# Keys of ten attention units transposed in 32 x 32 blocks by VectorE, and weight conversions started one chunk earlier

## The chip, the cores and the metric

The kernel runs on one core of a Trainium2 chip. The core has a matrix engine (TensorE, in the profile PE, with its weight loads as PEld), VectorE (DVE), ScalarE (ACT), GpSimd (POOL) and a queue engine (SyncE, SP) that here only issues DMAs; 16 DMA engines carry the transfers. TensorE writes into eight banks of PSUM, and VectorE or ScalarE take the results from there to SBUF. The metric is the device time of one execution in microseconds (us), the median of several runs.

## The reference

Everything is float32 at the boundary. Eight batches, 576 tokens, 8 heads of 64: a packed attention, then two mixing layers.

```python
p_packed = sm_attn(p, k, v)             # 32 packed queries p read 576 keys k
out = sm_attn(q, p_packed, p_packed)    # 576 queries q read the 32 packed rows
# sm_attn: softmax(q k^T / 8) v
x = out as [8, 576, 512]
xk, xr = mixes of x and of x one token earlier, by mu_k and mu_r
k = max(xk @ w_k, 0); v = (k * k) @ w_v; r = sigmoid(xr @ w_r); x = r * v
h = (x^T @ U @ V)^T; u = x + h
out = u + max(u @ w_ch1, 0) @ w_ch2     # 512 -> 2048 -> 512
```

The float64 weights (w_k, w_v, w_r, U, V, w_ch1, w_ch2) are converted to float32 on the chip, from their raw 64-bit words.

## The kernel before

**Attention units.** The batches go in four pairs, the heads in four pairs: 16 units, u = 4 * pair + head pair, each with two batches and two heads. A unit needs the keys K and queries Q with the 64 head dimensions on partitions, while a plain load puts tokens there. `attention_steps` (L664) works one unit: K into `kh` (and its last 64 tokens into `kt`), the packed queries into `pT`, scores of p against K, their exponentials `a1`, a product with V (`vin`), the packed result `pp`, then Q against `pp`, a second softmax `a2`, and the output `xo`, which is stored to `x_d` in DRAM.

There are two ways to turn an operand. The first is TensorE's transpose against the identity (`plan.transpose`, L207), 128 x 128 at a time into PSUM, and a copy out of PSUM by ScalarE or VectorE. The second is VectorE's transpose (`plan.turn`, L214), which transposes each 32 x 32 block in place; the load then has to bring the blocks to the right partitions, in pieces of 32 floats (128 B). `NPLAIN` (L522) is 8: units 0 to 7 turn K and Q by TensorE. In units 8 to 15 Q is already turned by VectorE (two transposes of 128 x 576) and `load_q` (L628) uses eight DMAs of 72 KB in 128-byte pieces; their final products run as three passes in a rounded format with zero-padded operands (`wide`) instead of full float32, and the second scores are computed transposed (`psat<-qt,ppt`). K is turned by TensorE in all 16 units: eight transposes of 128 x 128 and two of 64 x 128, two copies of 128 x 512 and one for the tail. `load_k` (L612) uses two DMAs of 256 KB and two of 32 KB.

**Chunks.** Phase 1 of the mixing layers runs in 12 chunks of 384 columns, three a pair of batches: `psr` (receptance), then eight `psk` and eight `psv` blocks, each product in three passes of a high and a low half. Chunks 0 to 2 read the output of units 0 to 3, chunks 3 to 5 that of units 4 to 7, and so on: the first chunk of a pair cannot start before its four units are stored and loaded again. Units 0 to 3 run alone at the start; the other twelve run between the chunks' matmuls. **Phase 2** (`psc`) is the last layer.

**Conversions.** `Cast.run` (L886) takes one [128, 512] block of 64-bit weights by one DMA of 512 KB into one of three buffers (`st`) and converts it with seven or eight instructions on ScalarE and VectorE. The weights of phase 1 (`wr`, `wk`, `wv`) are converted during the start and chunk 0, the last of them (`wv5` to `wv7`) just ahead of their use. The 34 blocks of U's partner V, `w_ch1` and `w_ch2` for phase 2 follow from the third chunk on, five a chunk (`CAST0, NPER = 2, 5`, L1385). From chunk 7 on `make_ws` (L1206) combines them into the operands of phase 2.

**Order.** All operations are first listed with their dependencies. `Plan.emit` (L346) then goes through them with modelled durations and writes, for each engine, one fixed order: the ready operation of the best class first, then by age or readiness. On the chip each engine runs its own order and waits at the head of its queue. In SP's order each DMA also waits for the DMA issued eight before it. A big buffer of a unit (`kin`, `qin`, `vin`, `kh`, `qt`, `at`, `th`, `xo`: eight, each reused one unit later) is loaded for unit u + 1 as soon as unit u has used it.

Of the kernel before, what the change touches and what calls it, by code (L numbers as in the profile page):

```python
# [9 lines left out]
F32 = mybir.dt.float32  # L10
# [3 lines left out]
AF = mybir.ActivationFunctionType  # L14
# [470 lines left out]
def packed_attention_moe_mixer_kernel(  # L485
# [18 lines left out]
    B, H, S, D = q.shape  # L504
    NP = p.shape[2]
    P = 128
    DM = H * D
    NJ = DM // P
# [10 lines left out]
    LATER = "v0 v1 v2 k0 k1 k2 k3 v3 v4 v5 v6 v7"  # L519
    NLEAD = NJ  # L520
    FIRST = "k0 p0 q0 w0 k1 v0 w1 q1 v1 w2 k2 q2 w3 v2 k3 w4 q3 v3 w5 w6 w7"
    NPLAIN = 2 * NJ  # L522
    SCALE = 1.0 / float(D) ** 0.5
    PASS = ((0, 0), (0, 1), (1, 0))

# [1 line left out]
    plan = Plan(nc)  # L527
# [37 lines left out]
    def ps_att():  # L565
        return plan.bank(att_banks[0], "psat", att_banks[0] is ps_a)
# [17 lines left out]
    class Bufs:  # L584
# [22 lines left out]
            return self.kept[1:]  # L607

        def tile_in(self, tag):
            return plan.tile(self.big_p, [P, 1152], F32, "big", parts=tuple(range(8)), name=tag)  # L610

        def load_k(self, u, after=()):  # L612
            bp, j = divmod(u, NJ)
            if u not in self.kin:
                self.kin[u] = self.tile_in("kin")
            t = self.kin[u]
            for b2 in range(2):
                src = k[2 * bp + b2, 2 * j:2 * j + 2]
                plan.dma(
                    t.at(b2)[:, b2 * 512:(b2 + 1) * 512].rearrange("p (h t d) -> p h t d", t=4, h=2),  # L620
                    src[:, 0:512, :].rearrange("h (p t) d -> p h t d", t=4), after=after)
            for b2 in range(2):
                src = k[2 * bp + b2, 2 * j:2 * j + 2]
                plan.dma(
                    t.at(2 + b2)[b2:P:2, 1024:1152].rearrange("p (h d) -> p h d", h=2),
                    src[:, 512:576, :].rearrange("h s d -> s h d"), after=after)

        def load_q(self, u, after=()):  # L628
# [3 lines left out]
            t = self.qin[u]  # L632
            if u >= NPLAIN:
                for b2 in range(2):
# [29 lines left out]
    def attention_steps(A, u, u_next):  # L664
        bp, j = divmod(u, NJ)
        kin, qin, vin = A.kin.pop(u), A.qin.pop(u), A.vin.pop(u)
        if j == 0 and bp + 1 < NBP:
            load_p(bp + 1)
        plan.copy(A.pbd, p_t[bp][:, j, :].unsqueeze(1).to_broadcast([P, 2, D]))
        plain = u < NPLAIN  # L670
        kh = A.big(F32, "kh")
        qt, at = A.big(F32, "qt"), A.big(F32, "at", (0, 1))
        pT, ppz = A.keep(plain)
# [5 lines left out]
        if early:  # L679
            claim()  # L680

        for b2 in range(2):
            yield
            ps = ps_att()
            for n in range(4):
                plan.transpose(ps[:, n * P:(n + 1) * P],
                               kin.at(b2)[:, b2 * 512 + n * P:b2 * 512 + (n + 1) * P], ident)
            plan.copy(kh[:, b2 * 512:(b2 + 1) * 512], ps)
        yield
        ps = ps_att()  # L690
        for h in range(2):
            plan.transpose(ps[0:64, h * P:(h + 1) * P], kin[:, 1024 + h * 64:1088 + h * 64], ident)
        plan.transpose(ps[:, 2 * P:3 * P], A.pbd.rearrange("p h d -> p (h d)"), ident)
        kt = at.at(1)[:, 640:896].rearrange("p (h c) -> p h c", h=2)
        plan.copy(kt[0:64].rearrange("p h (b c) -> p h b c", b=2),
                  ps[0:64, 0:2 * P].rearrange("p (h c b) -> p h b c", h=2, b=2))
        plan.copy(pT, ps[:, 2 * P:3 * P].rearrange("p (b c) -> p b c", b=2))
        if early:
            A.load_k(u_next, A.after)
# [1 line left out]
        st = A.st  # L701
        yield
        sps = [ps_att() for _ in range(2)]
        for b2 in range(2):
            for h in range(2):
                o = slice(b2 * 64 + h * 32, b2 * 64 + (h + 1) * 32)
                for r in range(2):
                    rows = slice(r * 64, (r + 1) * 64)
                    plan.mm(sps[r][o, 0:256], pT[rows, b2, h * 32:(h + 1) * 32],
                            kh[rows, b2 * 512 + h * 256:b2 * 512 + (h + 1) * 256],  # L710
                            start=True, stop=True, skip_group_check=True)
        for b2 in range(2):
            for h in range(2):
                o = slice(b2 * 64 + h * 32, b2 * 64 + (h + 1) * 32)
                plan.mm(sps[0][o, 256:320], pT[0:64, b2, h * 32:(h + 1) * 32],
                        kt[0:64, h, b2 * 64:(b2 + 1) * 64], start=True, stop=True, skip_group_check=True)
        s0, s1 = st.at(0), st.at(1)
        plan.reduce(s0[:, 0:1], sps[0][:, 0:320], ALU.max)
        plan.reduce(s0[:, 1:2], sps[1][:, 0:256], ALU.max)
# [1 line left out]
        a1 = A.a1  # L721
        bias = st.at(0)[:, 3:4]
        for r in range(2):
            plan.act(a1[:, 0:512].rearrange("p (n r c) -> p n r c", n=2, r=2)[:, :, r, :],
                     sps[r][:, 0:256].rearrange("p (n c) -> p n c", n=2), AF.Exp,
                     st.at(1)[:, 4 + r:5 + r], bias, SCALE)
        for b2 in range(2):
            r = slice(b2 * 64, (b2 + 1) * 64)
            plan.act(a1[r, 512 + b2:640:2], sps[0][r, 256:320], AF.Exp,
                     st.at(1)[r, 6:7], bias[r], SCALE)  # L730
        plan.reduce(s0[:, 8:9], s1[:, 4:8], add)
        plan.recip(s0[:, 9:10], s0[:, 8:9])

        for c in range(3 if plain else 0):
            yield
            ps = ps_att()
# [3 lines left out]
            n = 3 if c < 2 else 2  # L740
# [6 lines left out]
        if not plain:  # L747
            yield
            for b2 in range(2):
                r = slice(b2 * S, (b2 + 1) * S)  # L750
# [5 lines left out]
        ps = ps_att()  # L756
# [4 lines left out]
        ps = ps_att()  # L761
# [4 lines left out]
        ps = ps_att()  # L766
        for t in range(5):
            for g in range(4):
                o = t * P + g * 32
# [3 lines left out]
                        start=(t == 0), stop=(t == 4), skip_group_check=True)  # L773
# [3 lines left out]
        if not plain:  # L777
            for b2 in range(2):
                r = slice(b2 * 64, (b2 + 1) * 64)
# [5 lines left out]
        ps = ps_att()  # L785
# [13 lines left out]
        if plain:  # L799
# [25 lines left out]
            ps = ps_att()  # L825
# [4 lines left out]
            ps = ps_att()  # L830
            plan.transpose(ps[:, 0:P], a2f[:, 512:640], ident)
            for b2 in range(2):
                r = slice(b2 * 64, (b2 + 1) * 64)
                plan.copy(th[r, 512:576], ps[r, r])
        else:
            n = S // NP
            a2 = plan.tile(A.one, [P, 20, NP], F32, "a2", parts=(0, 1))[:, 0:n, :]
            s2 = plan.tile(A.one, [P, 4, 20], F32, "s2", parts=(0, 1))
            for g, (c0, c1) in enumerate(halves):
                yield  # L840
                ps = ps_att()
# [19 lines left out]
        for c0, c1 in halves:  # L861
            w = c1 - c0
            if plain:
                yield
                pss = [ps_att() for _ in range(2)]
                for b2 in range(2):
                    r = slice(b2 * 64, (b2 + 1) * 64)
# [13 lines left out]
    def attention(A, u, u_next):  # L881
        for _ in attention_steps(A, u, u_next):
            pass
# [83 lines left out]
    for what in FIRST.split():  # L967
        u = int(what[1])
# [14 lines left out]
    plan.cls = 0  # L983
    A0.after = go
    steps = [attention_steps(AX_[u], u, NJ if u == 0 else None) for u in range(NLEAD)]
    step = 0
    while any(s is not None for s in steps):
# [36 lines left out]
    for b2 in range(2):  # L1024
        r = slice(b2 * 64, (b2 + 1) * 64)
# [7 lines left out]
    for i0, i1 in ((0, NI),):  # L1033
        src = uv[:, i0 * NP:i1 * NP]
# [145 lines left out]
    def tmp_tile():  # L1180
        i = count["tmp"] % 6
        count["tmp"] += 1
        if i < 3:
            return plan.tile(m_p, [P, CW], F32, "m", name="tmp")[:, 0:256]
        return plan.tile(tr_p, [P, 256], F32, "tmp")
# [148 lines left out]
    def product(q, f, i, name, fresh):  # L1334

        if fresh:
            bank_abc[name] = plan.bank(ps_c1, "psc1")
        ps = bank_abc[name][:, 0:256]
        w, x = load_ws(f, i), ops[q][i]
        n = 0  # L1340
        for k in range(2):
            for wi, a in PASS:
                plan.mm(ps, half(w, wi)[:, k * P:(k + 1) * P],
                        half(x, a).rearrange("p (a k c) -> p k a c", a=4, k=2)[:, k],
                        start=(fresh and n == 0), stop=(n == 5), skip_group_check=True)
                n += 1
        return ps
# [34 lines left out]
            plan.dma(v_d[:, c * 288:(c + 1) * 288], w[0:NP, 0:288])  # L1382
        casts.append((slice(0, NP), V[:, c * 288:(c + 1) * 288], 288, put_v))
    NCAST, FIRST_WS = 9, 7
    CAST0, NPER = 2, 5  # L1385
    for m in range(MC):
        def put1(w, m=m):
            plan.dma(w1_d[m], w)
# [16 lines left out]
    for n in range(len(chunks)):  # L1405
        b, c = chunks[n]
# [27 lines left out]
        if n >= CAST0:  # L1434
            plan.cls = 3
            for _ in range(len(casts) if n == NCAST else NPER):
                if casts:
                    rows, src, size, put = casts.pop(0)
# [27 lines left out]
    for q in range(NQ):  # L1466
# [12 lines left out]
        for f in range(NF):  # L1479
# [9 lines left out]
            b = product(q, f, 1, "b", True)  # L1489
            s = tmp_tile()  # L1490
            plan.tt(s, p1, b, add)
            c = product(q, f, 2, "c", True)
# [68 lines left out]
```

## Time and profile before

| what | value |
|---|---|
| median of 3 runs | 1471.89 us (1470.66 to 1473.28) |
| profiled execution, its own time | 1469.44 us |
| span of that execution on the core | 1467.7 us |
| PE busy | 1434.1 us, 98% |
| PEld busy | 1259.5 us, 86% |
| DVE busy | 988.5 us, 67% |
| ACT busy | 716.2 us, 49% |
| mean granted TensorE clock | 0.988 |

1.74 us of the profiled execution lie outside its span. The page's slices show TensorE at 90% or more from the fourth slice to the last but one; a busy share is summed over modelled ends of pipelined matmuls, so it says that the engine had work, not how dense that work was. How dense is read from the distance between the start of a group of instructions and the start of the next group.

### The profile page before, as it was taken

The numbers are of one execution on the slowest core, as the hardware profiler recorded it, in microseconds if no ns is written. First come the engines' busy times: TensorE is split into PE (matmuls) and PEld (weight loads), VectorE is DVE, ScalarE is ACT, GpSimd is POOL, SyncE is SP. The second block draws the span as 40 slices with busy tenths as digits, with TensorE's granted clock in tenths as the row PEclk, the third lists the DMA queues.
The fourth block names the chain that finished last, engine by engine and source line by source line (L and its number), as shares of the span: only waits on it lengthen the run. The fifth ranks groups of instructions, "written<-read, shape, count | busy, mean of one in ns | idle before, by whom it ended". The sixth has DMA issues, their size and how long they took to land.

```text
span 1467.7 us, 25586 instructions
## 1 busy us (share of the span) xinstructions
PE 1434.1 (98%) x9104; PEld 1259.5 (86%) x9104; DVE 988.5 (67%) x2147; ACT 716.2 (49%) x1519; POOL 268.8 (18%) x519
## 2 busy tenths in 40 slices
PE   6799999999999999999999999999999999999998
PEld 5678888888888988889899999899998999999997
DVE  6999577888788888885665465556546554554533
ACT  5777656776666677664443333333223332333322
POOL 0000000000000000100333333333333333333331
PEclk8889999999999999999999999999999999999999
DMA  8864355666552877841999988899998789879763
GB/s 232 254 193 123 97 137 137 188 175 179 158 158 94 291 246 248 255 153 59 308 261 249 225 231 215 212 258 225 230 230 212 204 220 247 208 215 237 202 179 79
DMA packets 235709, 294.53 MB, mean 201 GB/s; under 512 B 91200, under 2 KB 126336, under 8 KB 235584
## 3 DMA queue, kind: packets, MB, share of 16 engines
q1 hardware_dynamic: 163008, 160.76, 37.8%
q0 software_dynamic: 72576, 132.15, 35.6%
q8 instruction: 73, 1.20, 0.3%
q14 instruction: 52, 0.43, 0.1%
HBM read 231.94 MB, written 60.89 MB: 200 GB/s over the span
## 4 chain that ended last, share of the span: by engine, by line
PE 90%; DMA 3%; DVE 3%; SPq 2%; ACT 1%; issue 1%; DVEq 0%; ACTq 0%
PE psc L197 50%; PE psk L197 13%; PE psv L197 13%; PE psr L197 7%; PE psat L197 4%; PE psat L209 2%; SPq L319 2%; PE psu L197 1%; DMA kin<-in_k_dram 1%; PE psh L197 1%; DMA st<-in_moe_w_k_dram 1%; DMA ut<-uq_d 0%; DMA st<-in_moe_w_v_dram 0%; DMA uq_d<-ux 0%; DMA w_d<-m 0%
## 5 line engine op out<-in xcount | busy, mean ns | idle before, releaser
L197 PE MATMUL psc<-w,hid 128*128 128x512 f32 x1728 | 421.1, 391 | 0.4 <-DVE hid L273 0.4
L197 PEld LDWEIGHTS psc<-ob,wb 128*128 128x128 f32 x3024 | 387.4, 191 | 13.4
L197 PE MATMUL psc<-ob,wb 128*128 128x256 f32 x3024 | 392.0, 283 | 0.0
L319 POOL DMA_DIRECT2D wb<-ws_d x504 | 266.9, 530 | 647.6 <-PE psc L197 401.5
L197 PEld LDWEIGHTS psc<-w,hid 128*128 128x128 f32 x1728 | 314.6, 188 | 60.6 <-DVE hid L273 1.5
L233 ACT ACTIVATE hid<-tmp 128x256 fp32r<-128x256 f32 x216 | 131.5, 676 | 231.0 <-DVE tmp L254 231.0
L197 PE MATMUL psk<-xk,wk 128*128 128x384 f32 x1152 | 227.1, 340 | 0.4 <-ACT sq L233 0.4
L197 PE MATMUL psv<-wv,kk 128*128 128x512 f32 x864 | 226.3, 397 | 0.0
L197 PEld LDWEIGHTS psk<-xk,wk 128*128 128x128 f32 x1152 | 201.3, 188 | 11.1 <-issue 2.6
L197 PEld LDWEIGHTS psv<-wv,kk 128*128 128x128 f32 x864 | 158.6, 188 | 32.9 <-issue 3.0
L273 DVE SCALAR_TENSOR_TENSOR hid<-tmp,hid 128x256 fp32r<-128x256 f32 x216 | 127.2, 633 | 54.6 <-ACT hid L233 54.1
L273 DVE SCALAR_TENSOR_TENSOR hid<-psc,hid 128x256 fp32r<-128x256 f32 x72 | 45.3, 629 | 167.4 <-ACT hid L233 167.4
L254 DVE TENSOR_TENSOR tmp<-tmp,psc 128x256 f32<-128x256 f32 x288 | 112.9, 409 | 61.7 <-PE psc L197 61.7
L233 ACT ACTIVATE hid<-psc 128x256 fp32r<-128x256 f32 x72 | 45.8, 636 | 157.3 <-PE psc L197 157.3
L197 PE MATMUL psr<-wr,xr 128*128 128x512 f32 x432 | 114.5, 406 | 2.0 <-DVE xr L291 1.6
L197 PEld LDWEIGHTS psr<-wr,xr 128*128 128x128 f32 x432 | 81.9, 194 | 21.3 <-DVE xr L291 2.1
L288 ACT ACTIVATE tmp<-psc 128x256 f32<-128x256 f32 x144 | 57.2, 397 | 58.7 <-PE psc L197 50.7
L233 ACT ACTIVATE sq<-psk 128x384 f32<-128x384 f32 x96 | 46.8, 489 | 75.1 <-PE psk L197 74.7
L311 POOL MEMSET x<- 128x8 f32 x4 | 0.4, 112 | 429.7 <-DVE m L270 249.2
L254 DVE TENSOR_TENSOR kk<-sq,kk 128x384 fp32r<-128x384 f32 x96 | 52.6, 549 | 25.1 <-ACT kk L288 24.6
L233 ACT ACTIVATE m<-x,om_t 128x384 f32<-128x384 f32 x96 | 55.3, 607 | 4.9 <-DVE xr L254 3.8
L270 DVE SCALAR_TENSOR_TENSOR m<-x,mu_t,m 128x384 f32<-128x384 f32 x96 | 56.4, 608 | 0.3 <-ACT m L233 0.2
(157 smaller groups left out, 1500.6 us busy)
## 6 DMA issues: line engine op xcount, KB each, us to landing
wb<-ws_d POOLq DMA_DIRECT2D x504, 256.0 KB, 4.0
st<-in_moe_w_ch_dram SPq DMA_DIRECT2D x32, 512.0 KB, 5.3
ws_d<-wb SPq DMA_DIRECT2D x56, 256.0 KB, 4.0
x_d<-xo SPq DMA_DIRECT2D x16, 576.0 KB, 3.8
x_d<-x SPq DMA_DIRECT2D x36, 256.0 KB, 2.6
kin<-in_k_dram SPq DMA_DIRECT2D x32, 256.0 KB, 4.5
vin<-in_v_dram SPq DMA_DIRECT2D x32, 256.0 KB, 4.8
x<-x_d SPq DMA_DIRECT2D x8, 1024.0 KB, 5.8
```

Of the source, the lines that this page charges most:

```text
L197: self.nc.tensor.matmul(o, l, r, start=start, stop=stop, **k)
L209: self.nc.tensor.transpose(out.get(), in_.get(), ident.get())
L233: self.nc.scalar.activation(o, in_.get(), func, **k)
L254: return self.elem(engs, lambda e, o, x, y: e.tensor_tensor(out=o, in0=x, in1=y, op=op), out, [a, b], self.TT, cls)
L270: ("dve",), lambda e, o, x, y, z: e.scalar_tensor_tensor(out=o, in0=x, scalar=z, in1=y, op0=op0, op1=op1), out, [a, b, s], {"dve": (1.042, ...
L273: ("dve",), lambda e, o, x, y: e.scalar_tensor_tensor(out=o, in0=x, scalar=s, in1=y, op0=op0, op1=op1), out, [a, b], self.TT, cls)
L288: self.nc.scalar.activation(o, i, AF.Copy)
L311: (self.nc.gpsimd if eng == "pool" else self.nc.vector).memset(o, 0.0)
L319: (self.nc.sync if eng == "sp" else self.nc.gpsimd).dma_start(out=o, in_=i)
```

## The change

`NPLAIN` goes from 8 to 6, so that the last ten units (6 to 15) are the second kind, and in that kind K is turned by VectorE as well. Q of units 6 and 7, with the second softmax and the final products, changes to the form that units 8 to 15 have; K changes in all ten. A K load of these units is 24 DMAs: 16 of 32 partitions x 8 x 32 floats (32 KB) and 8 of 32 x 2 x 32 floats (8 KB). One transpose of 128 x 1152 on VectorE replaces ten transposes on TensorE and three copies. The exponentials write in a permuted order to undo the load's. `CAST0, NPER` become 1, 4.

```diff
-    NPLAIN = 2 * NJ
+    NPLAIN = 6
         def load_k(self, u, after=()):
...
+            if u >= NPLAIN:
+                for b2 in range(2):
+                    for h in range(2):
+                        src = k[2 * bp + b2, 2 * j + h]
+                        main = src[0:512].rearrange("(p n r) (e s) -> r e p n s", p=32, r=2, e=2)
+                        c0 = (2 * b2 + h) * 256
+                        for g in range(4):
+                            plan.dma(t.at(8 * b2 + 4 * h + g)[g * 32:(g + 1) * 32, c0:c0 + 256]
+                                     .rearrange("p (n s) -> p n s", s=32), main[g // 2 ^ b2, g % 2], after=after)
+                        tail = src[512:S].rearrange("(p n) (e s) -> e p n s", n=2, e=2)
+                        c0 = 1024 + h * 64
+                        for e in range(2):
+                            g = 2 * b2 + e
+                            plan.dma(t.at(16 + 4 * b2 + 2 * h + e)[g * 32:(g + 1) * 32, c0:c0 + 64]
+                                     .rearrange("p (n s) -> p n s", s=32), tail[e], after=after)
+                return
...
-        for b2 in range(2):
+        for b2 in range(2 if plain else 0):
             yield
             ps = ps_att()
...
+        if not plain:
+            plan.turn(kh, kin)
         ps = ps_att()
-        for h in range(2):
+        for h in range(2 if plain else 0):
...
-                    rows = slice(r * 64, (r + 1) * 64)
+                    rows = r if plain else r ^ b2
+                    rows = slice(rows * 64, (rows + 1) * 64)
...
-    CAST0, NPER = 2, 5
+    CAST0, NPER = 1, 4
```

On TensorE the place is the start of unit 7. `kin` is its loaded K, `kh` its turned K, `th` and `pp` or `wide` the final products of unit 6, `pbd` the packed queries; the other rows are chunk matmuls. Before:

```order
L209 MATMUL psat_2323<-ident_118,kin_2035 128x128 x4
L209 MATMUL psat_2330<-ident_118,kin_2035 128x128 x4
L197 MATMUL psv_2024<-wv4_1111,kk_2162 128x512 x3
L209 MATMUL psat_2342<-ident_118,kin_2035 64x128 x2
L209 MATMUL psat_2342<-ident_118,pbd_151 128x128
L197 MATMUL psv_2025<-wv4_1111,kk_2162 128x512 x3
L197 MATMUL psk_2268<-xk_1781,wk0_1_1106 128x384 x3
L197 MATMUL psat_2364<-kh_2192,pT_216 32x256
```

And after the change, the same place:

```order
L197 MATMUL psat_2409<-th_2190,wide_153 128x256 x3
L197 MATMUL psk_2323<-xk_1815,wk0_0_204 128x384
L197 MATMUL psat_2414<-th_2190,wide_153 128x256 x3
L197 MATMUL psk_2323<-xk_1815,wk0_0_204 128x384 x2
L197 MATMUL psk_2323<-xk_1820,wk1_0_205 128x384 x3
L209 MATMUL psat_2440<-ident_118,pbd_151 128x128
L197 MATMUL psk_2323<-xk_2025,wk2_0_206 128x384 x3
L197 MATMUL psk_2323<-xk_2033,wk3_0_207 128x384 x3
L197 MATMUL psat_2455<-kh_2192,pT_1544 32x256
```

The ten transposes of `kin` are gone; of the unit's start only the transpose of `pbd` and the score products are left.

On VectorE the place is the end of chunk 0's weight conversions (`wv4`, `wv5`; `st` holds the raw words, `a` and `m` are scratch), while unit 5 is in work (`pp` is its packed result). Before:

```order
L273 SCALAR_TENSOR_TENSOR wv4_1111<-a_1531,st_1468 128x512
L254 TENSOR_TENSOR kk_1541<-sq_1422,kk_1541 128x384
L273 SCALAR_TENSOR_TENSOR m_1557<-st_1532,m_1557 128x512
L264 TENSOR_SCALAR a_1570<-a_1570 128x512
L277 TENSOR_REDUCE st_152<-st_152 128x1
L291 COPY qt_1266<-psat_1622 128x2x2x64
L264 TENSOR_SCALAR st_1532<-m_1557 128x512
L281 RECIPROCAL st_152<-st_152 128x1
L254 TENSOR_TENSOR kk_1582<-sq_1447,kk_1582 128x384
```

After:

```order
L273 SCALAR_TENSOR_TENSOR wv4_1111<-a_1552,st_1468 128x512
L277 TENSOR_REDUCE st_152<-st_152 128x1
L281 RECIPROCAL st_152<-st_152 128x1
L291 COPY at_1268<-psat_1662 128x512
L291 COPY at_1268<-psat_1667 128x128
L254 TENSOR_TENSOR kk_1603<-sq_1447,kk_1603 128x384
L270 SCALAR_TENSOR_TENSOR m_1680<-x_1299,mu_t_121,m_1680 128x384
L215 STREAM_TRANSPOSE kh_1709<-kin_1487 128x1152
L270 SCALAR_TENSOR_TENSOR pp_1450<-psat_1683,st_152,hmask_119 128x128
L254 TENSOR_TENSOR xr_1319<-m_1680,xr_1319 128x384
L291 COPY ppt_1267<-psat_1733 128x128
L264 TENSOR_SCALAR a_1591<-a_1591 128x512
```

The transpose of unit 6's K now stands directly ahead of unit 5's `pp`, and the first instruction on `wv5` (`a_1591`) has moved from ahead of these rows to behind them.

On SP the first place is the load of unit 6's K (`kin_1487`) among the last weight loads of chunk 0 (`st` from `w_v`). Before:

```order
L319 DMA st_1468<-in_moe_w_v_dram 128x1024
L319 DMA kin_1487<-in_k_dram 128x2x256 x2
L319 DMA kin_1487<-in_k_dram 64x2x64 x2
L319 DMA st_1532<-in_moe_w_v_dram 128x1024
L319 DMA st_1571<-in_moe_w_v_dram 128x1024
L319 DMA st_1616<-in_moe_w_v_dram 128x1024
L319 DMA qin_1631<-in_q_dram 64x18x64 x2
```

After:

```order
L319 DMA st_1468<-in_moe_w_v_dram 128x1024
L319 DMA kin_1487<-in_k_dram 32x8x32 x4
L319 DMA kin_1487<-in_k_dram 32x2x32 x2
L319 DMA kin_1487<-in_k_dram 32x8x32 x4
L319 DMA kin_1487<-in_k_dram 32x2x32 x2
L319 DMA kin_1487<-in_k_dram 32x8x32 x4
L319 DMA kin_1487<-in_k_dram 32x2x32 x2
L319 DMA kin_1487<-in_k_dram 32x8x32 x4
L319 DMA kin_1487<-in_k_dram 32x2x32 x2
L319 DMA st_1553<-in_moe_w_v_dram 128x1024
L319 DMA st_1592<-in_moe_w_v_dram 128x1024
L319 DMA qin_1644<-in_q_dram 32x18x32 x3
```

Twenty-four issues stand where four stood, ahead of the loads for `wv5`, `wv6` and `wv7`.

The second place on SP is the store of unit 7 (into `x_d1`) and the load of chunk 3's x from it. Before:

```order
L319 DMA x_d1_66<-xo_2520 128x1152
L319 DMA kin_2744<-in_k_dram 128x2x256 x2
L319 DMA kin_2744<-in_k_dram 64x2x64 x2
L319 DMA qin_2745<-in_q_dram 32x18x32 x8
L319 DMA x_2516<-x_d1_66 128x384
L319 DMA x_2516<-x_d1_66 128x2x63
```

After (`kin_2821`, `qin_2858` and `vin_3019` are unit 9's):

```order
L319 DMA kin_2821<-in_k_dram 32x2x32 x2
L319 DMA qin_2858<-in_q_dram 32x18x32 x8
L319 DMA x_d1_66<-xo_2621 128x1152
L319 DMA st_2935<-in_moe2_w_ch1_dram 128x4x256
L319 DMA w1_d2_80<-m_2504 128x512
L319 DMA w1_d3_81<-m_2650 128x512
L319 DMA vin_3019<-in_v_dram 128x2x256
L319 DMA vin_3019<-in_v_dram 64x2x64
L319 DMA vin_3019<-in_v_dram 128x2x256
L319 DMA vin_3019<-in_v_dram 64x2x64
L319 DMA x_2575<-x_d1_66 128x384
L319 DMA x_2575<-x_d1_66 128x2x63
```

Unit 9's K and Q have moved from behind unit 7's store to ahead of it, and unit 9's V now stands between that store and the last part of chunk 3's x.

## Rows read from the trace of the kernel before

**Rows 1.** Windows by stage: length, busy PE, PEld, DVE, ACT, POOL, clock, DMA share, GB/s.
```profile
106.00:253.00 147.00, 145.79 (x1005) 122.19 (x1004) 110.08 (x255) 94.24 (x207) 0.11 (x1) 1.00 0.44 125
253.00:476.00 223.00, 220.74 (x1551) 186.07 (x1550) 188.98 (x414) 150.80 (x335) 0.32 (x2) 1.00 0.55 160
476.00:690.00 214.00, 214.00 (x1058) 190.69 (x1057) 175.22 (x378) 141.58 (x294) 6.07 (x12) 1.00 0.64 212
690.00:1467.70 777.70, 771.03 (x4808) 696.36 (x4806) 424.41 (x884) 257.85 (x501) 260.98 (x493) 1.00 0.87 220
```

**Rows 2.** Timeline of PE, start of unit 5's K: start, length, instruction, count.
```profile
105.99 1.03 PE L209 MATMUL psat<-ident,kin 128*128 128x128 f32 x8
106.78 0.95 PE L197 MATMUL psk<-xk,wk 128*128 128x384 f32 x4
107.56 0.38 PE L209 MATMUL psat<-ident,kin 128*64 128x128 f32 x2
107.78 0.27 PE L209 MATMUL psat<-ident,pbd 128*128 128x128 f32 x1
```

**Rows 3.** Timeline of PE, the plain form of Q and the final products.
```profile
118.59 0.81 PE L209 MATMUL psat<-ident,qin 128*128 128x128 f32 x6
119.16 0.94 PE L197 MATMUL psv<-wv,kk 128*128 128x512 f32 x3
...
127.41 2.17 PE L197 MATMUL psat<-ppt,qt 128*128 128x64 f32 x18
129.34 0.42 PE L197 MATMUL psk<-xk,wk 128*128 128x384 f32 x1
...
102.06 0.96 PE L197 MATMUL psat<-th,pp 64*128 64x320 f32 x4
102.95 0.50 PE L197 MATMUL psv<-wv,kk 128*128 128x512 f32 x1
```

**Rows 4.** Timeline of PE, the same steps in unit 8's form.
```profile
234.59 1.19 PE L197 MATMUL psat<-qt,ppt 128*64 128x320 f32 x8 [0.74 <-ACT ppt L288]
235.71 0.44 PE L197 MATMUL psk<-xk,wk 128*128 128x384 f32 x1
...
247.96 0.75 PE L197 MATMUL psat<-th,wide 128*128 128x320 f32 x4
248.54 0.62 PE L197 MATMUL psv<-wv,kk 128*128 128x512 f32 x2
```

**Rows 5.** Tiles kh and qt: count, ns min/median/max, first and last start.
```profile
L288 ACT ACTIVATE kh<-psat x25: 580/597/618, 5.0 to 445.0; 128x512 f32<-128x512 f32 x25
L215 DVE STREAM_TRANSPOSE qt<-qin x16: 758/772/775, 202.5 to 441.5; 128x576 f32<-128x576 f32 x16
```

**Rows 6.** Timeline of SP, DMA issues: start, length, transfer, count.
```profile
106.62 2.70 SPq L319 DMA_DIRECT2D kin<-in_k_dram  x4
110.05 8.91 SPq L319 DMA_DIRECT2D st<-in_moe_w_v_dram  x3
...
187.55 5.38 SPq L319 DMA_DIRECT2D qin<-in_q_dram  x8
```

**Rows 7.** Tile kin: the issue of one DMA in ns, min/median/max, and its landing in us.
```profile
L319 SPq DMA_DIRECT2D kin<-in_k_dram x64: 379/608/1414, 0.7 to 414.4; - x64
...
DMA to landing us min/median/max: 2.6/4.3/6.9
```

**Rows 8.** Timeline of DVE, the last instruction on wv5, and of PE, its first use.
```profile
123.19 0.69 DVE L273 SCALAR_TENSOR_TENSOR wv<-a,st 128x512 fp32r<-128x512 f32 x1
...
131.01 4.28 PE L197 MATMUL psv<-wv,kk 128*128 128x512 f32 x18
```

**Rows 9.** Timeline of SP: the stores of units 6 and 7; of PE: chunk 3's first matmuls.
```profile
184.14 0.34 SPq L319 DMA_DIRECT2D x_d<-xo  x1
218.37 0.34 SPq L319 DMA_DIRECT2D x_d<-xo  x1
...
253.40 1.64 PE L197 MATMUL psr<-wr,xr 128*128 128x512 f32 x6
```

More of the change, by code (lines that the diff above doesn't have):

```diff
@@ L609, in tile_in @@
         def tile_in(self, tag):
-            return plan.tile(self.big_p, [P, 1152], F32, "big", parts=tuple(range(8)), name=tag)
+            return plan.tile(self.big_p, [P, 1152], F32, "big", parts=tuple(range(24)), name=tag)
         def load_k(self, u, after=()):
@@ L694, in attention_steps @@
         kt = at.at(1)[:, 640:896].rearrange("p (h c) -> p h c", h=2)
-        plan.copy(kt[0:64].rearrange("p h (b c) -> p h b c", b=2),
-                  ps[0:64, 0:2 * P].rearrange("p (h c b) -> p h b c", h=2, b=2))
+        if plain:
+            plan.copy(kt[0:64].rearrange("p h (b c) -> p h b c", b=2),
+                      ps[0:64, 0:2 * P].rearrange("p (h c b) -> p h b c", h=2, b=2))
         plan.copy(pT, ps[:, 2 * P:3 * P].rearrange("p (b c) -> p b c", b=2))
@@ L714, in attention_steps @@
                 o = slice(b2 * 64 + h * 32, b2 * 64 + (h + 1) * 32)
-                plan.mm(sps[0][o, 256:320], pT[0:64, b2, h * 32:(h + 1) * 32],
-                        kt[0:64, h, b2 * 64:(b2 + 1) * 64], start=True, stop=True, skip_group_check=True)
+                if plain:
+                    rows, tail = slice(0, 64), kt[0:64, h, b2 * 64:(b2 + 1) * 64]
+                else:
+                    rows = slice(b2 * 64, (b2 + 1) * 64)
+                    tail = kh[rows, 1024 + h * 64:1088 + h * 64]
+                plan.mm(sps[0][o, 256:320], pT[rows, b2, h * 32:(h + 1) * 32], tail,
+                        start=True, stop=True, skip_group_check=True)
         s0, s1 = st.at(0), st.at(1)
@@ L723, in attention_steps @@
         for r in range(2):
-            plan.act(a1[:, 0:512].rearrange("p (n r c) -> p n r c", n=2, r=2)[:, :, r, :],
-                     sps[r][:, 0:256].rearrange("p (n c) -> p n c", n=2), AF.Exp,
-                     st.at(1)[:, 4 + r:5 + r], bias, SCALE)
+            to, s = a1[:, 0:512].rearrange("p (n r c) -> p n r c", n=2, r=2)[:, :, r, :], sps[r][:, 0:256]
+            if plain:
+                s = s.rearrange("p (n c) -> p n c", n=2)
+            else:
+                to = to.rearrange("p n (c m) -> p m n c", m=4)
+                s = s.rearrange("p (m n c) -> p m n c", m=4, n=2)
+            plan.act(to, s, AF.Exp, st.at(1)[:, 4 + r:5 + r], bias, SCALE)
         for b2 in range(2):
             r = slice(b2 * 64, (b2 + 1) * 64)
-            plan.act(a1[r, 512 + b2:640:2], sps[0][r, 256:320], AF.Exp,
-                     st.at(1)[r, 6:7], bias[r], SCALE)
+            to, s = a1[r, 512 + b2:640:2], sps[0][r, 256:320]
+            if not plain:
+                to, s = to.rearrange("p (c m) -> p m c", m=2), s.rearrange("p (m c) -> p m c", m=2)
+            plan.act(to, s, AF.Exp, st.at(1)[r, 6:7], bias[r], SCALE)
         plan.reduce(s0[:, 8:9], s1[:, 4:8], add)
```

## The prediction, made before the changed kernel ran

> **What bounds the kernel now.** I read the windows by stage first. From 106 us, where the order of instructions begins to differ, to 476 us, where the attention units end, TensorE is busy 145.8 of 147.0 us and 220.7 of 223.0 us, at the full clock (1.00, the 2.4 GHz level) [rows 1]: 3.5 us of idle time in 370. From 476 to 690 us it is busy throughout. VectorE is busy 110.1 of 147 and 189.0 of 223 us, so 37 and 34 us of it are free; ScalarE has more. So phase 1 is a list of TensorE work without gaps, into which the twelve units from 4 on are threaded, and an instruction taken off TensorE should shorten the run by the room it took in that list, unless another engine or a queue cannot follow. The second view is the timeline of TensorE: matmuls overlap, so a group's price is the time from its start to the start of the next group, not its length. The third is SP's timeline, because the change multiplies its issues, and SP is a single queue.
>
> **What TensorE gets rid of.** *K, ten units.* Eight transposes of unit 5's K start at 105.99 and the next group at 106.78: 0.79 us; the two of the tail 0.22 us (107.56 to 107.78) [rows 2]. That is 1.01 us a unit, 10.1 us for ten.
>
> *Q of units 6 and 7.* Removed in each: nine transposes of Q, six of which take 0.57 us, so 0.86; the second scores, 18 instructions, 1.93 us; five transposes of `a2` at K's 0.79 / 8 = 0.10 us, so 0.49; the final products in float32, four of eight instructions in 0.89 us, so 1.78 [rows 2, 3]. Together 5.06 us. Added: the scores the other way round, 1.12 us, and twelve products with `wide`, four in 0.58 us, so 1.74 [rows 4]. Together 2.86. Net 2.2 us a unit, 4.4 for two. The score products against K keep their number and sizes; I cost their new row halves at nothing.
>
> TensorE's list is 14.5 us shorter. All of it lies inside the gapless stretch.
>
> The Trainium skill prices a transpose otherwise: its page "TensorE: Matmul & The Clock Gate", section "Part 4: PE-mode transpose", gives about 275 ns for 128 x 128 inside a kernel. A single transpose here does last 0.27 us, but eight take 0.79. At the page's price the 128 transposes that go (100 of K, 18 of Q, 10 of `a2`) would be worth 35 us instead of 12.8; as a rival this comes back below.
>
> **What VectorE and ScalarE get.** A turn of 128 x 1152 is not in the trace; the one of 128 x 576 takes 0.772 us [rows 5], so I take twice that, 1.54 (between 0.772, if only the fixed part counted, and 1.54, if none does). Ten of K and four half turns for each new Q unit's Q and `a2` add about 20 us at most; copies of 0.6 us go, most of them from ScalarE [rows 5]. VectorE has 71 us free between 106 and 476, so this hides; if it did not, 20 us is what it would cost. The conversions: the same 34, four a chunk from chunk 1 instead of five from chunk 2. Chunks 3 to 6 fill the 253 to 476 us window with twenty of them; even if all of VectorE's 189 us there were theirs, four would be under 38 us, which is what is free between 106 and 253. Four 512 KB loads in chunk 1 meet a DMA share of 0.44 [rows 1]. I cost this part at nothing.
>
> **What SP gets, and the one place where it hurts.** A K load is 24 issues instead of four. An issue of K takes 0.379 us at least, 0.608 in the median, 1.414 at most [rows 7]; eight issues of Q in the same 128-byte pieces take 5.38 us, 0.67 each [rows 6]. So 9.1 to 16.1 us instead of 2.70; I take the median, 14.6, since these pieces are smaller than Q's. For units 8 to 15 that fits: K 14.6, Q 5.4 and V about four medians, 2.4, are 22.4 us in a unit's pitch of 34 us (stores at 184.1 and 218.4) [rows 9], and each K is wanted some 25 us after its buffer came free.
>
> For unit 6 it does not fit as well. Its load starts at 106.6, as before, so its last piece lands 2.6 to 4.3 us after 121.2 [rows 6, 7]: at 123.8 to 125.5 (118.3 to 127.0 with the bounds). VectorE comes to the turn at about 122, since it used to end `wv5` at 123.9 and that work now stands behind [rows 8]. It waits 2 to 3 us, then turns for 1.5, and behind it stand unit 5's `pp`, chunk 1's first mixes and all of `wv5`. And the loads of `wv5` to `wv7` stand behind the 24 issues: `wv5` was ready 13.8 us after its load was issued (110.05 to 123.88) [rows 6, 8], so now at about 121.2 + 13.8 = 135, while TensorE took it up at 131.0 [rows 8]. Chunk 1's `psr` products are pulled in between, which covers part. I take a loss of 3.5 us, between 0 (9.1 us of issues: ready at 129.5) and 9 (16.1 us: ready at 136.5, and a wait for `pp` of 3.5 before).
>
> The Trainium skill, "DMA: Bandwidth & Descriptors", section "Why small descriptors are slow (HBM only)", charges about 3 cycles a packet beside one per 32 bytes. From the old K load's 2.70 us that makes an estimate of 4.3 us for the same 576 KB in 128-byte pieces, K would land near 114, and the sum would be the full 14.5 us, 1457. No run here shows such a K load; Q's eight issues speak for the queue's pace instead.
>
> **The sum.** 14.5 - 3.5 = 11.0 us off the profiled execution's 1469.4, so 1458.4; the median of the runs is 2.5 us above that execution, so 1461.
>
> **Rivals.** *Chunk 3 waits for unit 7 (no change).* The store of unit 7 now stands behind unit 9's K and Q, and the last part of chunk 3's x behind unit 9's V, which waits for unit 8's product with V. If SP takes K and Q up only when unit 7 is done (218.4), the store leaves at 238, V holds the queue to about 250, and x is loaded and mixed at 256, where chunk 3 would have begun at 253.4 - 6.4 = 247 [rows 9]. That costs 9 us more: 1470. Against it: K and Q wait only for unit 8's turns, so most of those 20 us should run before 218.
>
> *SP is the pace (slower).* Each DMA waits for the one eight before. If an issue of K's pieces takes the longest row, 1.41 us, K needs 33.9 us, `wv5` is ready at 106.6 + 33.9 + 13.8 = 154, and TensorE loses 23 us at 131: 1472 - 14.5 + 23 = 1480. It turns slower from 1.05 us an issue (106.6 + 24 x 1.05 + 13.8 - 131 = 14.6). For it: a landing of up to 6.9 us. Against: 6.9 / 8 is 0.86, and Q's bigger pieces run at 0.67.
>
> *A transpose costs its whole length (much faster).* At 0.27 us each [rows 2] the 128 are worth 34.6 instead of 12.8 us: 1439. Against it stand the start times. The page on TensorE named above is the one that would have it so.
>
> **How the numbers follow.** The forecast with its losses of 0 to 9 us: 0.74. Chunk 3 waits: 0.10. SP is the pace: 0.08. Whole length: 0.02. Something else that loses the gain: 0.06, half of it slower. The likeliest is 1461. The range starts at 1454 (14.5 us and the 3.5 us of idle time, both gone) and ends at 1468 (a loss of 9 in chunk 0 and 1.5 more elsewhere); 0.18 is left out. No change means within 0.2%, 2.9 us, about what a measurement of this kernel can tell. Faster: 0.74 + 0.02 + 0.06 of the chunk 3 case that costs less than its full price + 0.01 = 0.83; same 0.07; slower 0.10.
>
> **What would show it.** Right: no transposes of `kin` or `qin` after unit 5; chunk 3's `psr` near 245 instead of 253; TensorE still without gaps from 160 to 690; a `kin` issue near 0.6 us; one wait of a few us between 122 and 145, of VectorE for `kin` or of TensorE for `wv`. Wrong: TensorE idle over 10 us in 106 to 253, or SP busy without a gap from unit to unit with `x` behind it, or phase 2's start not some 11 us earlier.

## The result: 21 us slower

The changed kernel takes 1492.78 us (median of four, 1489.09 to 1494.47) against 1471.28 (1466.59 to 1473.28) for the kernel before: a ratio of 1.0147, with a 95% interval of 1.0116 to 1.0179. The prediction was 1461, faster. The profiled execution has a span of 1487.3 us and a time of 1489.09, 19.65 above the one of before.

Windows of the changed kernel by stage, columns as in [rows 1]:

```profile
106.00:253.00 147.00, 129.54 (x881) 107.59 (x880) 112.59 (x252) 86.32 (x194) 0.11 (x1) 0.97 0.52 127
253.00:476.00 223.00, 208.45 (x1431) 171.31 (x1429) 181.97 (x386) 141.36 (x312) 0.11 (x1) 0.98 0.58 156
476.00:690.00 214.00, 214.00 (x1057) 190.29 (x1054) 180.09 (x387) 142.46 (x296) 6.37 (x13) 1.00 0.65 213
```

TensorE was idle 3.5 us between 106 and 476 us in the kernel before; now it is idle 17.5 + 14.5 = 32.0, and the granted clock is no longer 1.00. The first product of phase 2, before and after, in TensorE's timelines (start, length, instruction, count):

```profile
690.89 0.52 PE L197 MATMUL psc<-ob,wb 128*128 128x256 f32 x3
```
```profile
709.66 0.52 PE L197 MATMUL psc<-ob,wb 128*128 128x256 f32 x3
```

It starts 18.8 us later, so nearly all of the 19.65 us is lost in phase 1. TensorE's timeline after, around its longest idle time; the bracket is the idle time before the row and what ended it:

```profile
140.22 1.21 PE L197 MATMUL psr<-wr,xr 128*128 128x512 f32 x4 [1.90 <-ACT xr L288]
...
155.60 1.65 PE L197 MATMUL psv<-wv,kk 128*128 128x512 f32 x3 [11.07 <-ACT wv L288]
...
296.27 0.90 PE L197 MATMUL psat<-th,wide 128*128 128x320 f32 x2 [4.07 <-ACT th L233]
...
329.26 2.21 PE L197 MATMUL psr<-wr,xr 128*128 128x512 f32 x6 [4.18 <-ACT xr L288]
```

The profile names ScalarE's copy `wv` as the releaser. ScalarE's own timeline shows why it was late:

```profile
142.32 0.62 ACT L233 ACTIVATE m<-x,om_t 128x384 f32<-128x384 f32 x1 [1.01 <-DVE xr L254]
154.07 0.46 ACT L233 ACTIVATE a<-st 128x288 f32<-128x288 f32 x1 [11.13 <-DMA st<-in_moe_U_dram]
154.43 0.60 ACT L233 ACTIVATE m<-x,om_t 128x384 f32<-128x384 f32 x1
154.93 0.61 ACT L288 ACTIVATE wv<-m 128x512 fp32r<-128x512 f32 x1
```

The first instruction of U's conversion stood at the head of ScalarE's queue for 11.13 us, waiting for U's raw words, which TensorE first uses at 171.4 us (`psu`). The copy that ends `wv7`, two places behind it, could not pass. The SP rows of the same time say where U's load was:

```profile
105.27 16.56 SPq L319 DMA_DIRECT2D kin<-in_k_dram  x24
121.93 1.76 SPq L319 DMA_DIRECT2D st<-in_moe_w_v_dram  x2
...
132.10 2.65 SPq L319 DMA_DIRECT2D vin<-in_v_dram  x4
134.85 15.48 SPq L319 DMA_DIRECT2D kin<-in_k_dram  x24
150.44 1.18 SPq L319 DMA_DIRECT2D st<-in_moe_U_dram  x2
151.71 5.55 SPq L319 DMA_DIRECT2D qin<-in_q_dram  x8
```

It stood behind the 24 issues of unit 7's K and left at 150.44. In the kernel before, the same row is:

```profile
124.48 1.19 SPq L319 DMA_DIRECT2D st<-in_moe_U_dram  x2
```

Later the same wait returns with other loads: in the view of waits (engine, tile and line, what it waited for: sum us, times, longest), after and then before:

```profile
ACT a L233 <- DMA st<-in_moe_w_ch_dram: 22.6, 6, 7.9
ACT a L233 <- DMA st<-in_moe_U_dram: 11.1, 1, 11.1
```
```profile
ACT a L233 <- DMA st<-in_moe_w_ch_dram: 6.2, 6, 2.7
```

Behind these stand the copies `th` and `xr` for which TensorE is idle at 296 and 329. For the one at 329, SP's rows show the load of w_ch behind a K load (SP had no idle time between the two rows), and ScalarE's rows the wait with `xr` behind it:

```profile
296.09 16.99 SPq L319 DMA_DIRECT2D kin<-in_k_dram  x24
...
322.27 0.56 SPq L319 DMA_DIRECT2D st<-in_moe_w_ch_dram  x1
```
```profile
328.13 0.66 ACT L233 ACTIVATE a<-st 128x512 f32<-128x512 f32 x1 [7.92 <-DMA st<-in_moe_w_ch_dram]
328.69 0.51 ACT L288 ACTIVATE xr<-m 128x384 fp32r<-128x384 f32 x1
```

Each long idle time also costs clock, as these windows of the changed kernel show (length, busy PE, clock, DMA share, GB/s); the clock is back at 1.00 from 165 and from 300:

```profile
145.00:155.00 10.00, 0.00 (x0) 0.71 0.38 72
155.00:165.00 10.00, 8.73 (x53) 0.78 0.76 209
...
290.00:300.00 10.00, 5.93 (x25) 0.83 1.05 332
```

### The profile page after: what moved, and what is told of

Read it like the earlier page. It is cut to its first block, busy times and chain, and to the rows that moved or that the text cites. A ratio compares the mean times of both kernels' runs of the same rounds, so it can differ in the third digit from the quotient of the medians.

```text
span 1487.3 us, 25545 instructions
## 1 busy us (share of the span) xinstructions
PE 1427.5 (96%) x8964; PEld 1249.6 (84%) x8964; DVE 998.5 (67%) x2143; ACT 710.1 (48%) x1507; POOL 268.9 (18%) x519
## 2 busy tenths in 40 slices
DMA packets 282110, 294.54 MB, mean 198 GB/s; under 512 B 142720, under 2 KB 172736, under 8 KB 281984
## 4 chain that ended last, share of the span: by engine, by line
PE 83%; DMA 6%; SPq 4%; DVE 4%; ACT 1%; issue 1%; DVEq 0%; ACTq 0%
PE psc L197 47%; PE psk L197 12%; PE psv L197 11%; PE psr L197 6%; SPq L319 4%; PE psat L197 4%; PE psat L209 1%; DMA vin<-in_v_dram 1%; DMA ut<-uq_d 1%; DMA uq_d<-ux 1%; PE psu L197 1%; PE psh L197 1%; DMA st<-in_moe_w_ch_dram 0%; DMA kin<-in_k_dram 0%; DMA st<-in_moe_w_r_dram 0%
## 5 line engine op out<-in xcount | busy, mean ns | idle before, releaser
L197 PE MATMUL psk<-xk,wk 128*128 128x384 f32 x1152 | 223.9, 339 | 0.2 <-ACT sq L233 0.2
L254 DVE TENSOR_TENSOR tmp<-tmp,psc 128x256 f32<-128x256 f32 x288 | 113.0, 409 | 62.4 <-PE psc L197 62.4
L254 DVE TENSOR_TENSOR kk<-sq,kk 128x384 fp32r<-128x384 f32 x96 | 52.5, 551 | 28.0 <-ACT kk L288 27.7
L233 ACT ACTIVATE a<-st 128x512 f32<-128x512 f32 (+2 forms) x55 | 36.1, 656 | 51.2 <-DMA st<-in_moe_w_ch_dram 22.6
```

The lines of the kernel that those rows point to most:

```text
L197: self.nc.tensor.matmul(o, l, r, start=start, stop=stop, **k)
L233: self.nc.scalar.activation(o, in_.get(), func, **k)
L254: return self.elem(engs, lambda e, o, x, y: e.tensor_tensor(out=o, in0=x, in1=y, op=op), out, [a, b], self.TT, cls)
```

## The experiments

All comparisons are with the kernel before on the same chip; a ratio is given with its 95% interval in brackets. `Plan.emit` writes the fixed order of each of these kernels anew, so an edit can also move instructions that it does not name; no run holds the order fixed. Theory A (called so in what was expected) is the one that the trace suggests: a K load now holds SP for about 16 us, so other loads come late, and in-order engines wait for them with urgent work behind.

**One wait taken away, and the order's assumption changed.** In the first kernel U's words go into a buffer that lies idle then (`xs`), so their load need not wait for a conversion buffer:

```diff
-            cv.run([(slice(0, 64), src), (slice(64, P), src)], NI * NP, put_u, after=after)
+            cv.run([(slice(0, 64), src), (slice(64, P), src)], NI * NP, put_u, after=after, own=xs_p)
```

> The changed kernel, but the raw words of U get a buffer of their own (that of xs, which is idle until then), so that their load is issued ahead of unit 7's K instead of behind it; nearly nothing else in the order moves. Theory A (SP's 24 issues a unit take 0.65 to 0.85 us each, the order was made for 0.5, and a weight conversion at the head of ScalarE's queue waits for its late load while work of the critical path stands behind it): the wait of 11.1 us before wv7's products goes, with the half clock behind it, so 10 to 16 us faster than the changed kernel, 1477 to 1483; the waits at 296, 329, 393 and 428 us stay. Rival B (128-byte pieces clog the DMA engines and everything lands late): under 4 us faster, since as many pieces move and wv7 would be late anyway, 1489 to 1493. Rival C (conversions started a chunk earlier are what costs): no change, 1490 to 1494.

Measured: 1483.43 us (1482.37 to 1488.10), ratio 1.0088 [1.0063, 1.0113]: 13.1 us slower than before in place of 21.5. The 8.4 us gained are fewer than the 10 to 16 that theory A asked for. The wait of 11 us is gone, and another has come (the profiled execution is the slowest of the four, 1488.10 us):

```profile
411.20 0.90 PE L197 MATMUL psat<-th,wide 128*128 128x320 f32 x2 [9.54 <-ACT th L233]
```

So that wait was real, but it is one of several of its kind. The second kernel leaves the work alone and makes the order with 650 ns of queue time for a DMA instead of 500:

```diff
-    LEAD = (60.0, 500.0, 1.0, 1700.0)
+    LEAD = (60.0, 650.0, 1.0, 1700.0)
```

> The changed kernel, but the list scheduler that writes the fixed order counts 650 ns of queue time for each DMA instead of 500; same instructions, another order. Theory A: the order then fits the queue, most of the 32 us of TensorE idle time between 106 us and phase 2 goes, idle under 10 us, 1458 to 1470. Rival B: the transfers themselves are slow, later positions of single instructions help little, idle over 20 us, 1480 to 1495. Rival C: as many conversions as early, 1485 or more.

Measured: 1486.01 us (1485.51 to 1486.21), 1.0098 [1.0076, 1.0121]. The idle times that TensorE's timeline shows before phase 2 sum to 18 us in place of 31, but phase 2 then starts with waits for VectorE. A better estimate gives back some 6 us, at the edge of what the two intervals can tell apart, and a K load still holds SP for 15.8 to 19.7 us. Theory A had expected 1458 to 1470 and missed; the time lies in the ranges of rivals B and C.

**Fewer issues, same pieces.** Each K load as 12 DMAs of 64 partitions:

```diff
-                        for g in range(4):
+                        for g in range(2):
...
-                                     .rearrange("p (n s) -> p n s", s=32), main[g // 2 ^ b2, g % 2], after=after)
+                            plan.dma(t.at(8 * b2 + 4 * h + g)[g * 64:(g + 1) * 64, c0:c0 + 256], main[g ^ b2],
+                                     after=after)
...
```

> The changed kernel, but a K load of units 6 to 15 is 12 DMAs of 64 partitions instead of 24 of 32; the same bytes in the same 128-byte pieces. Theory A (issues count): K takes about half the queue time, 8 to 10 us a unit, TensorE idle under 12 us between 106 us and phase 2, 1458 to 1472. Rival B (pieces count): K takes about as long, 13 to 17 us a unit, 1485 to 1495. Rival C: the same, 1485 to 1495.

Measured: 1546.7 us (1544.8 to 1550), 1.0514 [1.0489, 1.0539]. SP's timeline:

```profile
106.72 23.95 SPq L319 DMA_DIRECT2D kin<-in_k_dram  x12
```

Half as many issues took 24 us instead of 16.6, 2.0 us each, and the time lies outside all three expectations. So the number of issues alone does not set the time that SP spends on a K load; with more of that time everything got worse (ScalarE waited 62.4 us for w_ch, VectorE 37.1 us, in five waits, for K itself). The number of pieces in an issue does not set it either: a turned Q is the same 576 KB in the same 128-byte pieces, in eight issues of 576 pieces, and took 5.55 us in the rows above, 0.69 each. In the source pattern of the 12 the slowest dimension is the two halves of a row (`e`), in that of the 24 and of Q's eight it is 32 groups of tokens; whether this makes the difference was not tried.

**The conversions back to the third chunk, five a chunk** (`CAST0, NPER = 2, 5`):

> The changed kernel, but the phase-2 conversions as before the change: from the third chunk on, five a chunk. Theory A: U's wait of 11 us stays, and so do waits for conversion loads behind K; within 8 us of the changed kernel, 1485 to 1498. Rival B: the same. Rival C (the early conversions cost the time): 1458 to 1466.

Measured: 1498.02 us (1494.03 to 1501.30), 1.0180 [1.0153, 1.0206]. The early conversions are not the cost, and rival C falls: without them the changed kernel is no faster (27.7 us slower than before against 21.5, with intervals that overlap).

**Load and turn apart.** These two decide it. In the first, the kernel before gets only the new load, and TensorE turns what lands:

```diff
+            if u >= 6:
+                for b2 in range(2):
...
-                               kin.at(b2)[:, b2 * 512 + n * P:b2 * 512 + (n + 1) * P], ident)
+                               kin[:, b2 * 512 + n * P:b2 * 512 + (n + 1) * P], ident)
```

> The kernel before, with nothing changed but the load of K in units 6 to 15: it takes the 24 DMAs in 128-byte pieces of the changed kernel, and TensorE still turns what lands (so K of these units holds scrambled keys and the output is not the reference's). TensorE's list of work is the one of before. Theory A (the queue time of the 24 issues puts other loads late, and engines wait for those at the head of their queues): 20 to 35 us slower than before, 1490 to 1505, with ScalarE waiting over 5 us for raw weight words (st) more than once and K loads of 15 to 17 us on SP. Rival T (the loss comes from the turns on VectorE and the new order of the units, not from the load): within 5 us of before, 1466 to 1475.

Measured: 1516.40 us (1513.96 to 1519.11), 1.0322 [1.0303, 1.0342], 46.8 us slower. The signs that theory A named are there: ScalarE waits 28.6 us for w_ch, in seven waits of up to 6.3 us, and K holds SP for 16.4 to 17.5 us. The edit also lets each transpose of K wait for the whole load instead of one batch's half, but TensorE waited for `kin` 4.2 us in sum, against 6.6 before. In the second, the changed kernel keeps all but its load (the `if u >= NPLAIN` branch of `load_k` is gone):

> The changed kernel with everything in place except the load of K, which is the four DMAs of before (the blocks land in the wrong places, so the output is not the reference's). Theory A: the gain that was forecast without its loss in chunk 0: 10 to 15 us faster than before, 1455 to 1461, TensorE idle under 8 us between 106 us and phase 2. Rival T: still slower than before, 1480 or more.

Measured: 1460.88 us (1459.92 to 1461.24), 0.9940 [0.9925, 0.9955]. The windows of the load alone, then of the turn with the old load:

```profile
106.00:253.00 147.00, 138.51 (x957) 113.91 (x955) 98.62 (x225) 90.86 (x206) 0.11 (x1) 1.00 0.46 115
253.00:476.00 223.00, 199.25 (x1328) 166.23 (x1329) 161.20 (x347) 131.37 (x292) 0.12 (x1) 0.94 0.53 139
```
```profile
106.00:253.00 147.00, 146.41 (x992) 122.82 (x991) 129.42 (x288) 101.55 (x224) 0.11 (x1) 1.00 0.54 150
253.00:476.00 223.00, 217.85 (x1476) 181.50 (x1474) 196.48 (x420) 153.44 (x330) 0.32 (x2) 1.00 0.58 171
```

The rival, that VectorE's turns and the new order cost the time, falls: with them and the old load TensorE is idle 5.7 us, and phase 2 starts at 679.29, 11.6 us earlier than before. The load by itself makes TensorE idle 32 us and lowers the mean clock to 0.94 in 253 to 476 us. Its price exceeded the expected 20 to 35. Of the 11.6 us, 2.1 are lost again in phase 2, which lasts 778.9 us instead of 776.8; why stays open.

**Q alone.** The kernel before with `NPLAIN = 6` for Q and the early conversions, K as it was:

> The kernel before with Q of units 6 and 7 turned by VectorE and the conversions from chunk 1, four a chunk; K stays on TensorE with four DMAs a unit. Both theories leave this part its 4.4 us of TensorE's list: 1464 to 1468. If the earlier conversions or the Q part cost something of their own, 1472 or more.

Measured: 1465.36 us (1464.18 to 1469.85), 0.9975 [0.9961, 0.9989], 4.25 us faster: the forecast 4.4 within the interval.

**The queue moved.** The changed kernel with K's DMAs issued by GpSimd's queue:

```diff
-                                     .rearrange("p (n s) -> p n s", s=32), main[g // 2 ^ b2, g % 2], after=after)
+                                     .rearrange("p (n s) -> p n s", s=32), main[g // 2 ^ b2, g % 2], after=after, eng="pool")
...
```

> The changed kernel with the 24 DMAs of each K issued by GpSimd's queue instead of SP's; pieces, bytes and turns are the same. Theory A: SP is free for the other loads, the waits of ScalarE for raw weight words fall under 6 us in sum, and the time falls by 15 us or more against the changed kernel, to 1460 to 1478 (the upper end if a K lands late because GpSimd issues more slowly). Rival B (23,040 more small pieces slow the transfers themselves): the waits stay and the time is 1485 to 1495.

Measured: 1461.95 us (1461.51 to 1462.30), 0.9948 [0.9933, 0.9963]. GpSimd needs nearly as long for the 24, and SP now sends U's words at 123.33:

```profile
123.36 14.29 POOL L319 DMA_DIRECT2D kin<-in_k_dram  x24 [23.78 <-ACT xr L288]
```
```profile
117.58 5.65 SPq L319 DMA_DIRECT2D qin<-in_q_dram  x8
123.33 2.13 SPq L319 DMA_DIRECT2D st<-in_moe_U_dram  x2
```

ScalarE's waits for w_ch and U are no longer among the first sixty rows of the view of waits. So the loss goes with the shared queue. Two other things change with it. K is also loaded earlier (unit 6's from 81.79 us instead of 105.27), but in the changed kernel VectorE waited for K's data only once, 3.80 us. And the profile counts K's pieces in fewer and larger packets there (last section), so this run alone does not exclude rival B. Against B stand the landings: from issue to landing a block of w_ch took 5.5 us in the median in the changed kernel and 5.3 before, the store of a converted block 5.4 and 4.5; that is up to about 1 us, where ScalarE waited 11. (With the old load the packets under 512 B are 96,000, with the new one 142,720: 46,720 more, not 23,040.) The Trainium skill, "DMA: Bandwidth & Descriptors", section "Issuing engines are not separate DMA queues", says that issuing from several engines only saves the sequencers' issue time, usually small beside the transfer. Here that time was not small, some 16 us of SP for each K load, and the move was worth 29 us in all (21.5 slower against 7.7 faster).

**What stands behind K.** The raw words of U, V, w_ch1 and w_ch2 on GpSimd's queue instead, K on SP:

```diff
-                plan.dma(to, src, after=after)
+                plan.dma(to, src, after=after, eng="pool" if raw and parts is None else "sp")
```

> The changed kernel with the raw words of U, V, w_ch1 and w_ch2 loaded through GpSimd's queue; K's 24 issues stay on SP, and the loads of wv5 to wv7 stay behind them. Theory A1 (the loss is conversions whose load stands behind K, waited for at the head of ScalarE's queue): the waits for U and w_ch fall to under 6 us in sum, and what is left is chunk 0's wait for wv and the K and x loads: 1464 to 1475. Theory A2 (SP's load makes K, Q, V, the stores and x themselves late): 1480 or more, with waits of VectorE or TensorE for kin, qin or x in place of ScalarE's for st.

Measured: 1475.47 us (1473.78 to 1478.52), 1.0041 [1.0028, 1.0054], at the upper edge of A1. K's pieces and their queue are those of the changed kernel, so 16 of the 21.5 us were the loads of conversions behind K. In the rest there is another link of the same chain, which the first reading had missed; VectorE, TensorE, then SP:

```profile
341.95 0.77 DVE L215 STREAM_TRANSPOSE qt<-a 128x576 f32<-128x576 f32 x1
350.93 0.43 DVE L264 TENSOR_SCALAR m<-a 128x512 int32<-128x512 int32 x1 [8.21 <-DMA w_d<-m]
...
352.21 0.75 DVE L254 TENSOR_TENSOR th<-qt,th 128x576 fp32r<-128x576 f32 x1
```
```profile
353.02 1.44 PE L197 MATMUL psat<-th,wide 128*128 128x320 f32 x4 [6.89 <-DVE th L254]
```
```profile
319.82 10.52 SPq L319 DMA_DIRECT2D kin<-in_k_dram  x15
330.46 6.68 SPq L319 DMA_DIRECT2D qin<-in_q_dram  x8
...
343.61 1.16 SPq L319 DMA_DIRECT2D w_d<-m  x2
```

The store of a converted block (`w_d<-m`) left SP at 343.61, behind K, Q and V. Until it had landed, the next conversion could not write `m`; VectorE waited for that 8.21 us with `th` behind, and TensorE 6.89 us for `th`. Of the waits that rival A2 named, VectorE has one for kin, 3.9 us, about the 3.80 of the changed kernel, and TensorE's for kin are 5.9 us in sum (6.6 before). The view also puts 8.3 us of ScalarE's `xo` down to kin, but the product that `xo` copies began only at 353.02, after the wait for `th`.

**Half the issues, and two more.** K's second batch on GpSimd's queue (`eng="pool" if b2 else "sp"`):

> The changed kernel with the twelve DMAs of K's second batch on GpSimd's queue and the other twelve on SP's. Theory A: a K load takes about 8 us of SP instead of 16, and the time lies between the changed kernel (1493) and the one with all of K on GpSimd (1462), nearer the latter: 1461 to 1472. If every issue on SP costs in proportion: 1477.

Measured: 1458.31 us (1456.56 to 1462.28), 0.9929 [0.9904, 0.9954], the lowest median here. SP's part of a K load:

```profile
105.45 8.72 SPq L319 DMA_DIRECT2D kin<-in_k_dram  x12
```

Not 1477, as a proportional price has it, and below theory A's 1461: with about 8 us less on SP per unit the loss is gone entirely. Phase 2 starts at 678.32, as early as with the old load.

> The kernel with K on GpSimd's queue, and the eight DMAs of each turned Q there as well (32 issues a unit, about 18.6 us of 34 at 0.58 each). Theory A: SP was no longer the limit with K gone, so 1459 to 1464, no measurable difference from K alone; if Q behind K on one queue comes late, 1466 or more.

K and Q both on GpSimd's queue: 1481.36 us (1480.62 to 1482.00), 1.0076 [1.0059, 1.0094]. The time is lost in the last units: TensorE runs half empty from 400 to 440. On GpSimd the last K ends at 404.7 (18 issues from 394.58) and the last Q's eight start at 414.62, after 9.95 idle us for which the view names no wait; what held them was not tried.

> The kernel with K on GpSimd's queue, and the order made with 0.65 us of queue time for each DMA instead of 0.5. Theory A: the issues measured 0.58 there, so the fixed order fits the chip a little better and TensorE's 7.6 us of idle time in phase 1 shrinks to what the kernel before has, 3.5: 1457 to 1462. If the order is as good already: 1460 to 1464.

K on GpSimd, order made with 650 ns: 1458.72 us (1458.67 to 1460.20), 0.9925 [0.9907, 0.9942]; without it 0.9948, and the intervals overlap. TensorE's idle time hardly fell (7.6 to 6.7 us): inconclusive.

## Why the prediction was wrong

**The step that failed** is "For units 8 to 15 that fits", with its sum of 22.4 us in a pitch of 34 [rows 9] and "each K is wanted some 25 us after its buffer came free". The sum was nearly right (16 for K, 5.5 for Q and 2.7 for V are 24), and K did arrive in time: VectorE's only notable wait for it was the forecast one. But fitting in a pitch says that SP keeps up on the average, not that the load behind K is in time. Those loads, and the stores of converted blocks, were priced at nothing: the paragraph on the conversions holds their loads only against a DMA share of 0.44 and ends "I cost this part at nothing". What waits for them stands in an in-order queue with TensorE's next operand behind it: 11.13 us of ScalarE for U's words became 11.07 us of TensorE.

**Rows that would have told it** were at hand: the new order of SP puts U's two DMAs behind unit 7's K, and the DMAs of w_ch behind K and Q of later units. The prediction followed SP's list only to `wv5`. The loss of 3.5 us, bounds 0 to 9, became 32.0 - 3.5 = 28.5 us of TensorE idle. One of the prediction's own signs of being wrong came, TensorE idle over 10 us in 106 to 253 (17.5), and another, a start of phase 2 that is not 11 us earlier (18.8 later).

**What was right.** With the old load phase 2 begins 11.6 us earlier although TensorE is idle 2.3 us more than before: the list is 13.9 us shorter (forecast 14.5). The sum after is then -13.9 + 28.5 = 14.6, and 18.8 was lost; the other 4.2 us would fit the lower clock (0.97 of 147 us and 0.98 of 223 are 8.9 us, part of it in the idle time itself), which no run tests. That several kernels without the loss land near 1461 is in part luck: the forecast had 3.5 us of loss in it, and not the 2.1 us that the turn with the old load loses in phase 2. The load's own figures: K of unit 6 took 16.56 us (14.6 taken, 16.1 the bound: its DMAs are smaller than Q's but took as long each, 0.69 us), a transpose of 128 x 1152 took 1.37 (1.54 taken), VectorE's wait was 3.80 us (2 to 3 taken; TensorE then waited 2.77 for `pp`), and `wv5` was ready at 134.83 + 0.65 = 135.5 (135 taken):

```profile
L319 SPq DMA_DIRECT2D kin<-in_k_dram x264: 385/607/1778, 0.7 to 442.9; - x132
...
L215 DVE STREAM_TRANSPOSE kh<-kin x10: 1358/1374/1378, 124.6 to 448.9; 128x1152 f32<-128x1152 f32 x10
```
```profile
124.60 1.38 DVE L215 STREAM_TRANSPOSE kh<-kin 128x1152 f32<-128x1152 f32 x1 [3.80 <-DMA kin<-in_k_dram]
...
134.83 0.65 DVE L273 SCALAR_TENSOR_TENSOR wv<-a,st 128x512 fp32r<-128x512 f32 x1
```

**The rivals.** "SP is the pace" had the right queue and the wrong price: it asked for 1.05 us an issue, at `wv5` alone, and 0.69 was enough, because more than `wv5` stood behind. "Chunk 3 waits for unit 7" did not come: TensorE is busy 53 of 53 us from 200 to 253, and chunk 3's first `psr`, at 258.05 instead of near 245, follows the matmuls before it without a wait. "A transpose costs its whole length" would have made the turn with the old load over 30 us faster, and it was 8.7. The estimate of 4.3 us for a K load, worked out in the prediction from the Trainium skill ("DMA: Bandwidth & Descriptors", "Why small descriptors are slow (HBM only)"), stands against 16.56 measured on the queue. It scaled the 2.70 us of SP's issues by what the page says of transfers; what the transfers alone took is not separated here.

**Still open:** why the load alone costs 46.8 us while it costs the full change about 30 (21.5 and the 8.7 not gained), what the rest of the loss is made of when the conversions' loads are out of the way (5.4 us slower than before, where the old load is 8.7 faster), and why 64-partition issues are so slow.

## What to carry to other kernels

When a change multiplies the DMAs on a queue, do not stop at "it fits in the period": walk the queue's new order and ask of every load and store that now stands behind the burst who waits for it, and what stands behind that waiter on its own engine. A load that nobody needs urgently becomes urgent once it sits at the head of an in-order queue in front of work that is. Before giving up the gain, split the burst over two queues: in this kernel half of K's issues elsewhere turned 1.5% slower into 0.7% faster, while K and Q together on the other queue lost again.

## What the runs showed of the hardware

- The 24 issues of a K load (16 of 256 pieces of 128 B, 8 of 64) held SP 0.69 us each for unit 6 (16.56 / 24; 15.5 to 20.2 us a load over the ten units) and GpSimd 0.60 (14.29 / 24); in 12 issues (8 of 512 pieces, 4 of 128) they held SP 2.0 us each for unit 6. Q's eight issues of 576 such pieces held SP 0.69 each (5.55 / 8).
- The same K pieces appear differently by queue: packets under 512 B were 142,720 with K on SP and 96,640 with K on GpSimd, where the queue's count rose by 7,680, which is 32 for each of the 240 DMAs.
- TensorE's granted clock fell to 0.71 in the ten idle microseconds after 145 us and was 0.78 in the next ten, with TensorE busy again; from 400 to 440 us of the kernel with K and Q on GpSimd it was 0.61 and then 0.50 (the 1.2 GHz level) while TensorE was busy 18.6 of 40 us.
